# Attention decode with backward: one 2 MB store per outer product instead of two of 1 MB, and the V evacuation behind the p copy

## The chip, the cores and the metric

The kernel runs on one core of a Trainium2 chip. The metric is the device time of one execution in microseconds (us); each result was compared with runs of the kernel before on the same chip in the same rounds. The 16 DMA engines of the core play the main part. In the traces every transfer of the queue leaves 16 completion marks, one per engine, and the marks come in the order in which the transfers were issued: in the kernel before, none of 3328 marks lies ahead of the mark of the same rank of the transfer before it. So the text treats each engine as working through its own share in that order.

## The reference, cut to what matters

```python
B, H, Sq, Skv, Dh = 1, 32, 1, 8192, 128          # bf16
scores = einsum('bhqd,bhkd->bhqk', q, k) * Dh ** -0.5
attn   = softmax(scores)
out    = einsum('bhqk,bhkd->bhqd', attn, v)
# returned: out, and the gradients of q, k, v for a given grad_out
```

With one query row per head, the gradients of k and v are outer products: dk is ds times q, dv is p times grad_out, each as large as K itself. So a head reads K and V (2.1 MB each) and writes dk and dv (2.1 MB each), and does little arithmetic per byte.

## The kernel before: the parts concerned

The store of an outer product. VectorE makes a quarter per call (r = 0 to 3); after every second quarter a DMA of 1 MB is issued, 128 rows of 8 KB. The last head stores in quarters. All DMAs go through one queue (SyncE), in program order.

```python
NST = 2
def outer(h, which, r):
    ...
    nc.vector.tensor_tensor(slots(G, r, 4) ..., op=ALU.mult)
    parts = 4 if h == H - 1 else NST
    if r % (4 // parts) == 4 // parts - 1:
        c = r // (4 // parts)
        nc.sync.dma_start(rows_of(dst, h, c, parts), slots(G, c, parts))
```

The order of a head h (p_ is the head before). The K transpose `k_blocks(h + 1, 0)` waits for the next K load, and VectorE executes in this order, so dk's third and fourth quarters stand behind that wait:

```python
    k_scores(h); v_transposes(h, 1)
    ds_of(p_); outer(p_, "dk", 0); s_mask(h); s_swap(h); outer(p_, "dk", 1)
    k_blocks(h + 1, 0)                    # VectorE: waits for K of head h + 1
    ... mx, diag ...
    outer(p_, "dk", 2); outer(p_, "dk", 3); dq_of(p_)
    load_k(h + 2)                         # needs the buffer that dq_of frees
    ...
    v_transposes(h, 3)                    # 16 transposes on PE, one 1 us copy on ScalarE
    rinv = ...                            # VectorE
    x["p"] = ...                          # ScalarE: the p copy
    v_scores(h, 2); contract(Vt.pop(h), x["p"], ...)
    for r in range(4): outer(h, "dv", r)
    ...
    load_v(h + 2)
```

## Time and profile before

| | before |
|---|---|
| time, median of the first 3 runs | 674.32 us (672.83 to 674.49) |
| span of the profiled run | 672.6 us |
| one turn (head) in the middle | 20.45 us |
| DMA rate in the middle (164 to 629 us) | 410 GB/s |
| from the landing of the last K to the end | 43.4 us |

The lines behind this table stand in the prediction. One view more matters for what follows, the list of DMA issues: out<-in, engine, operation, count, KB of each, median us from issue to landing.

```profile
out_dram<-G_dv SPq DMA_DIRECT2D x62, 1024.0 KB, 11.8
out_dram<-G_dk SPq DMA_DIRECT2D x62, 1024.0 KB, 11.9
Vt<-in_v_dram SPq DMA_DIRECT2D x30, 2048.0 KB, 16.4
```

A landing here is the completion of the 16 engines. A 1 MB store needs about 2.5 us of an engine's time (8 packets of 309 ns).

### The profile page before, as it was taken

The numbers are of one execution on the slowest core, as the hardware profiler recorded it, in microseconds if no ns is written. First come the engines' busy times: TensorE is split into PE (matmuls) and PEld (weight loads), VectorE is DVE, ScalarE is ACT, GpSimd is POOL, SyncE is SP. The second block draws the span as 40 slices with busy tenths as digits, with TensorE's granted clock in tenths as the row PEclk, the third lists the DMA queues.
The fourth block names the chain that finished last, engine by engine and source line by source line (L and its number), as shares of the span: only waits on it lengthen the run. The fifth ranks groups of instructions, "written<-read, shape, count | busy, mean of one in ns | idle before, by whom it ended". The sixth has DMA issues, their size and how long they took to land.

```text
span 672.6 us, 23041 instructions
## 1 busy us (share of the span) xinstructions
PE 524.4 (78%) x10727; PEld 483.7 (72%) x10727; DVE 508.7 (76%) x658; ACT 172.4 (26%) x321; POOL 0.7 (0%) x6
## 2 busy tenths in 40 slices
PE   3788897878888787878787887878787888877783
PEld 3687786767777777777777777767777777777682
DVE  4678896777787877877777778768777678687766
ACT  1323322222222223222222222222222222222320
POOL 0000000000000000000000000000000000000000
PEclk9975656565555555555555555656556565566665
DMA  8899999999999999999999999999999999999976
GB/s 338 370 382 422 419 427 418 422 427 424 405 410 414 409 411 393 421 416 402 406 412 405 413 413 409 402 416 409 423 419 399 423 399 415 413 396 417 391 292 252
DMA packets 29808, 269.96 MB, mean 401 GB/s; under 512 B 3472, under 2 KB 3472, under 8 KB 6032
## 3 DMA queue, kind: packets, MB, share of 16 engines
q1 hardware_dynamic: 29712, 268.48, 97.6%
q8 instruction: 84, 1.38, 0.8%
q14 instruction: 12, 0.10, 0.0%
HBM read 134.23 MB, written 134.23 MB: 399 GB/s over the span
## 4 chain that ended last, share of the span: by engine, by line
DMA 64%; PE 23%; DVE 8%; ACT 3%; issue 1%; SPq 1%; ACTq 0%; DVEq 0%
DMA Kt<-in_k_dram 64%; PE dp_ps L185 8%; PE T_ps L168 5%; DVE XK_sb L133 5%; PE m_ps L256 3%; PE dp_ps L180 3%; ACT XT_sb L170 2%; PE m_ps L185 1%; PE s_ps L145 1%; DVE diag L254 1%; DVE G_dv L195 1%; DVE G_dk L195 1%; PE m_ps L276 0%; DVE mx L252 0%; ACT p_rep L282 0%
## 5 line engine op out<-in xcount | busy, mean ns | idle before, releaser
L168 PE MATMUL T_ps<-ident,Vt 128*128 128x128 bf16 x2048 | 238.3, 310 | 1.1 <-DMA Vt<-in_v_dram 1.1
L168 PEld LDWEIGHTS <-Vt 128*128 128x128 bf16 x2048 | 218.5, 150 | 7.0 <-issue 5.4
L170 ACT COPY XT_sb<-T_ps 128x1024 f32<-128x1024 f32 x128 | 129.5, 1012 | 334.2 <-PE T_ps L168 334.2
L195 DVE TENSOR_TENSOR G_dv<-p_rep,qd 128x2048 bf16<-128x2048 bf16 x128 | 148.2, 1221 | 77.5 <-ACT p_rep L282 63.4
L133 DVE STREAM_TRANSPOSE XK_sb<-Kt 128x1024 f32<-128x1024 f32 x128 | 155.1, 1230 | 57.2 <-DMA Kt<-in_k_dram 57.2
L195 DVE TENSOR_TENSOR G_dk<-ds_rep,qd 128x2048 bf16<-128x2048 bf16 x128 | 153.2, 1219 | 1.1
L180 PEld LDWEIGHTS <-XT_sb 128*128 128x128 bf16 x2048 | 72.5, 106 | 45.1 <-ACT XT_sb L170 43.8
L180 PE MATMUL dp_ps<-doT,XT_sb 128*128 128x1 bf16 x2048 | 75.1, 166 | 35.3 <-ACT XT_sb L170 35.3
L185 PE MATMUL m_ps<-p_rep,Vt 128*128 128x1 bf16 x2048 | 59.0, 165 | 37.0 <-ACT p_rep L282 37.0
L185 PEld LDWEIGHTS <-Vt 128*128 128x128 bf16 x2048 | 59.5, 104 | 39.0 <-issue 39.0
L145 PE MATMUL s_ps<-q_blk,XK_sb 128*128 128x4 bf16 x2048 | 59.1, 168 | 0.0
L185 PE MATMUL dp_ps<-ds_rep,Kt 128*128 128x1 bf16 x2048 | 58.2, 164 | 0.7 <-issue 0.5
L145 PEld LDWEIGHTS <-XK_sb 128*128 128x128 bf16 x2048 | 57.1, 104 | 0.0
L185 PEld LDWEIGHTS <-Kt 128*128 128x128 bf16 x2048 | 56.2, 101 | 0.8 <-issue 0.6
L256 PE MATMUL m_ps<-diag,ones_f 128*128 128x128 f32 x64 | 21.5, 431 | 38.1 <-DVE diag L254 38.1
L256 PEld LDWEIGHTS m_ps<-diag,ones_f 128*128 128x128 f32 x64 | 13.9, 270 | 45.1 <-DVE diag L254 45.1
L276 PEld LDWEIGHTS m_ps<-rs,ones_f 128*128 128x128 f32 x64 | 15.9, 309 | 25.2 <-ACT qd L211 25.2
L276 PE MATMUL m_ps<-rs,ones_f 128*128 128x1 f32 x64 | 18.6, 360 | 16.4 <-ACT qd L211 16.4
L224 ACT COPY dq_all<-dp_ps 128x1 f32<-128x1 f32 x32 | 5.1, 159 | 93.4 <-PE dp_ps L185 93.4
L151 DVE TENSOR_TENSOR sm<-s_ps,in_quad 128x256 f32<-128x256 f32 x32 | 13.6, 425 | 12.3 <-PE s_ps L145 12.3
L287 ACT COPY o_all<-m_ps 128x1 f32<-128x1 f32 x32 | 5.1, 159 | 61.8 <-PE m_ps L185 61.8
L291 PE MATMUL m_ps<-o_all,do_f 128*128 128x1 f32 x64 | 18.1, 352 | 0.0
(40 smaller groups left out, 160.2 us busy)
## 6 DMA issues: line engine op xcount, KB each, us to landing
Kt<-in_k_dram SPq DMA_DIRECT2D x31, 2048.0 KB, 15.9
out_dram<-G_dv SPq DMA_DIRECT2D x62, 1024.0 KB, 11.8
out_dram<-G_dk SPq DMA_DIRECT2D x62, 1024.0 KB, 11.9
Vt<-in_v_dram SPq DMA_DIRECT2D x30, 2048.0 KB, 16.4
Vt<-in_v_dram SPq DMA_DIRECT2D x8, 512.0 KB, 11.2
Kt<-in_k_dram SPq DMA_DIRECT2D x4, 512.0 KB, 5.2
out_dram<-G_dv SPq DMA_DIRECT2D x4, 512.0 KB, 3.4
out_dram<-G_dk SPq DMA_DIRECT2D x4, 512.0 KB, 4.6
```

Source lines behind the costliest of these rows:

```text
L133: nc.vector.transpose(XK[h][:, :, :, u, :], slots(Kt[h], u, NCH).rearrange("p g d -> p (g d)").bitcast(F32).rearrange("p (g w j) -> p g w ...
L145: nc.tensor.matmul(out[:, g, :], lhsT=cols[:, g, c // 2, c % 2], rhs=q_blk[:, h, c, :], start=(c == 0), stop=(c == 2 * NB - 1), skip_group ...
L151: nc.vector.tensor_tensor(x["sm"][:], x["s"][:, 0:NT].rearrange("p (a g) -> p a g", a=NQ).unsqueeze(2) .to_broadcast([P, NQ, NCH, CH]), in ...
L168: nc.tensor.transpose(T_ps[:, i, :], Vt[h][:, c * CH + i, :], ident[:])
L170: nc.scalar.copy(X.rearrange("p c s -> p (c s)").bitcast(F32), T_ps.rearrange("p c s -> p (c s)").bitcast(F32))
L180: nc.tensor.matmul(st[h]["dp"][:, n:n + 1], lhsT=X[:, i, :], rhs=doT[:, h:h + 1], start=True, stop=True, skip_group_check=True)
L185: nc.tensor.matmul(out_col, lhsT=Xt[:, n, :], rhs=rep[:, n, 0:1], start=(n == 0), stop=(n == NT - 1), skip_group_check=True)
L195: nc.vector.tensor_tensor(slots(G, r, 4).rearrange("p n (a b) -> p n a b", b=R), slots(rep, r, 4).unsqueeze(2).to_broadcast([P, Q, D // R, ...
L254: nc.vector.tensor_scalar(diag[:], ident_f[:], mx[:], scale, op0=ALU.mult, op1=ALU.mult)
L256: nc.tensor.matmul(x["m"][:, 128:256], lhsT=ones_f[:], rhs=diag[:], start=True, stop=True, skip_group_check=True)
L276: nc.tensor.matmul(x["m"][:, 0:1], lhsT=ones_f[:], rhs=rs[:], start=True, stop=True, skip_group_check=True)
L291: nc.tensor.matmul(x["m"][:, 1:2], lhsT=do_f[:, h:h + 1].to_broadcast([P, P]), rhs=o_all[:, h:h + 1], start=True, stop=True, skip_group_ch ...
```

## The change

Fewer and longer stores, and p earlier. The one part halves the number of store packets and DMAs; the other lets the p copy, on which V's contraction and the dv products wait, go ahead of a V evacuation on ScalarE.

```diff
-NST = 2
+NST = 1
@@
-        v_transposes(h, 3)
         rinv = small.tile([P, 1], F32, tag="rinv")
         ...
         x["p_s"] = small.tile([P, NT], F32, tag="p_s", name="p_s")
         nc.vector.tensor_scalar(x["p_s"][:], e[:], rinv[:], scale, op0=ALU.mult, op1=ALU.mult)
+        v_transposes(h, 3)
         v_scores(h, 2)
```

## The prediction

> **What bounds the kernel now.** I read the row of slices and the DMA queues on the page first, then the chain of waits in time order for two heads in the middle, then the busy time by stage, then the timeline of one head and of the last two.
>
> ```profile
> PE   3788897878888787878787887878787888877783
> ...
> DVE  4678896777787877877777778768777678687766
> ...
> DMA  8899999999999999999999999999999999999976
> ...
> q1 hardware_dynamic: 29712, 268.48, 97.6%
> ```
>
> No compute engine is full (PE and DVE stay at 6 to 8 tenths in all but one of the slices between the ends), the 16 DMA engines are at 9 from the third slice to the 38th, and the one data queue fills 97.6% of them. The chain that ended last says the same of a middle head:
>
> ```profile
> 304.74 15.76 DMA Kt<-in_k_dram
> 320.49 0.02 issue
> 320.52 1.25 DVE XK_sb L133
> 321.76 0.12 DVE mx L252
> 321.88 0.02 issue
> 321.91 0.30 DVE diag L254
> 322.20 0.04 issue
> 322.25 0.80 PE m_ps L256 x2
> 323.05 0.40 PE dp_ps L180 x16
> 323.45 1.71 PE dp_ps L185 x64
> 325.16 0.03 PE m_ps L207
> 325.19 15.85 DMA Kt<-in_k_dram
> ```
>
> One turn is 20.45 us: a 2 MB K load is issued and lands 15.8 us later, 4.7 us of compute follow until dq has freed a K buffer, and the next load goes out. The load takes so long because other transfers lie ahead of it in the queue: a head moves K, V, dk and dv, 8.39 MB, and 8.39 MB in 20.45 us is 410 GB/s. So a turn is DMA throughput, not latency. By stage (columns: PE, PEld, DVE, ACT, POOL busy us and instructions, then clock, DMA share, GB/s):
>
> ```profile
> 0.00:28.00 28.00, 14.05 (x225) 12.32 (x226) 13.04 (x28) 6.51 (x9) 0.70 (x6) 1.00 0.92 372
> 28.00:42.00 14.00, 12.37 (x276) 11.61 (x273) 13.62 (x18) 3.21 (x5) 0.00 (x0) 1.00 0.87 309
> 42.00:98.00 56.00, 47.51 (x994) 44.62 (x994) 46.22 (x60) 16.01 (x30) 0.00 (x0) 0.53 1.01 423
> 98.00:164.00 66.00, 51.20 (x1043) 47.19 (x1040) 49.84 (x64) 16.75 (x34) 0.00 (x0) 0.55 1.01 423
> 164.00:629.00 465.00, 372.56 (x7605) 343.26 (x7603) 356.52 (x450) 121.11 (x225) 0.00 (x0) 0.53 1.01 410
> 629.00:672.60 43.60, 26.75 (x604) 24.74 (x601) 29.42 (x41) 8.82 (x19) 0.00 (x0) 0.58 0.74 295
> ```
>
> The reader is to see two limits. From 42 to 629 us the DMA share is 1.01: only faster packets help there. From 629 us, where the last K has landed, the share is 0.74 and the chain is compute: a shorter path helps there. Between 28 and 42 us, when the first loads are done and the first outputs are not there yet, the DMA also waits a little (0.87).
>
> **What the Trainium skill says.** "DMA: Bandwidth & Descriptors", section "Why small descriptors are slow (HBM only)", gives each packet a fixed overhead of about 3 cycles and a fixed descriptor cost. The packet records of this trace agree that there is one and that it is small here: the median packet of 4096 bytes takes 159 ns, of 8192 bytes 309 ns, of 16384 bytes 611 ns. That is 150 ns per 4096 bytes plus about 9 ns per packet. The section "Rules for kernel authors" asks for 128 partitions and at least 1 MiB per DMA for full bandwidth; the stores before (1024 KB each in the list of DMA issues) already have that, so no jump is promised. The section "Where 436 GB/s comes from" puts the ceiling at 435.2 GB/s; the 423 of the best stage is 3% under it, so there is little above. "Perfetto Trace Analysis", section "Per-engine timelines", calls ScalarE a strict FIFO; the trace agrees: the p copy starts at 308.84 us, right behind a V evacuation at 307.93 us, though its scalar from the reciprocal was written at 306.55 us.
>
> **The change, part by part.** *Stores.* In 31 of 32 heads (the last stores in four parts before and after) dk and dv go from two 1 MB DMAs each to one of 2 MB. An engine writes 8 of the 128 rows, so per head it handles 32 packets of 8192 bytes before and 16 of 16384 after. The size of 16384 occurs only in loads before; I choose to apply the same law to stores, because the stores of 8192 lie on the line through the other two. Then 32 x 309 = 9888 ns become 16 x 611 = 9776 ns: 112 ns less. Two DMAs fewer also save two semaphore packets of 9 ns on each engine: 18 ns. Sum 130 ns per head, x 31 = **4.0 us**, all of it in the stretch that DMA bounds. The trigger moves: dv's first half waits for two more products (2 x 1.2 = 2.4 us), dk's for a K transpose and two products (318.85 to 324.4: 5.6 us). Does the queue run dry? The V load issued at 314.47 us takes 16.4 us to land, that is until 331, so the queue holds work when dk comes at 324.4; K, issued at 304.74 and landing at 320.5, covers dv at 314. No. The order of bytes in the queue (dv, V, dk, K) stays.
>
> *Buffers.* An output tile is rewritten two heads (41 us) later; a store landing some 14 us after its later issue is long done. No new wait. SBUF does not change.
>
> *V evacuation behind p.* The number of instructions is the same on every engine and the order on PE is the same; only on ScalarE do the 1.01 us copy (row of L170: 1012 ns) and the 0.51 us p copy change places, and on VectorE nothing but tags moves. The p copy no longer waits for 16 transposes (1.87 us) and the evacuation: it can start at about 306.6 instead of 308.84, so VectorE's dv products start 2.3 us earlier. On PE the contraction with V waited for p until 309.40; now it waits only for the scores before it, which end at 308.24: 1.15 us earlier. In the DMA-bound stretch both lie beside the transfers: zero. In the last 43.6 us they lie on the chain twice. Head 30: 1.15 us through PE. Head 31: here the chain runs from p into VectorE's eight products to the end, and VectorE stood idle for 2.74 us, so 2.3 us. The end of the chain moves by about 3.4 us; the DMA must then push out dk of head 30 (2 MB, one store at about 650) and 4 MB of head 31 by then: 6.3 MB at 410 GB/s are 15.4 us, so about 666, against some 669.5 before. Both agree; I take **3.3 us**.
>
> *Start.* dv of head 0 goes out at about 30.0 whole instead of 29.57 and 32.19 in halves, and V2 behind it some 2 us earlier. The gap from 28.3 us grows by 0.5, the later small gaps (0.4 at 36, 0.35 at 41 us) close, and the low rate around 35 to 42 us may improve: **0.5 to 1 us** gained.
>
> Sum: 4.0 + 3.3 + 0.7 = 8.0 us, 674.3 - 8.0 = 666.3 us.
>
> **The rivals.** (a) *Slow packets decide.* The loads' mean packet is 648 ns against the median 611, the stores' (8192) 316 against 309: 7892 x 37 / 16 + 15890 x 6.6 / 16 = 25 us per engine are spent in slow packets. From 98 to 164 us there are hardly any and the rate is 423; after 164 us, where half of the engines load while the other half store, it is 410. If the longer packets or the fewer DMA boundaries keep the engines in the good state, 465 us x (1 - 410/423) = 14 us more are saved: 652 us. If 16 KB stores get slow as often as the loads do (6% instead of 2% of some 305 us of store packets), 12 us are lost, and the time is 678. Nothing in the profile tells which; I think neither, as bytes and order in the queue stay. (b) *Later triggers starve the queue* (dk 5.6 us later). Against it is the backlog of some 14 us at K's issue; for it, only the start and the end, where there is no backlog: at the end dk of head 30 as one store leaves DMA idle from 646 to 650. That would eat 2 to 3 us of the tail: 669. (c) *The evacuation behind p becomes a wait*: scores of the fourth V part need it. They come on PE after the contraction of 1.84 us, and the evacuation ends about 308.9, before that: no wait. (d) *PE or DVE as bound*: in the first 98 us a head took about 18.5 us by the same chain, so compute allows 18.5 us against DMA's 20.45; the change only lowers it. No.
>
> **Range and chances.** The certain terms are small: packets 4, tail 2 to 3.5, start 0 to 1. The uncertain one is (a), some 12 us either way with about one chance in six for a large part of it, more likely as a gain since fewer and longer transfers are less mixed. The 2% line is 660.8 us, 5.5 us under my number, and needs a visible gain in slow packets. I give 0.17 to faster, 0.80 to same, 0.03 to slower, and a range of 656 to 673.
>
> **What would show it.** Right: store packets of 16384 bytes with a median near 611 ns; half of the store issues at 2048 KB; a middle turn of 20.3 us with K still waited for; DMA share still 1.01 with 411 to 414 GB/s in the middle; the p copy ahead of the evacuation and the contraction 1.15 us earlier against the row sums' matmul; some 40 us instead of 43.6 from the last K landing to the end. Wrong: a middle rate far from 410 (then rival a, to be seen in mean minus median of the packets), DMA share under 1.0 in the middle (rival b), or a new wait of PE on the evacuation (rival c).

## The result and the profile after

The changed kernel is slower: 681.52 us in the median of 4 runs (679.74 to 683.2), the kernel before 674.4 us. The ratio is 1.0106 with a 95% interval of 1.0073 to 1.0140. That is within 2%, but clear of noise, outside the predicted range, and on the other side.

The page of the changed kernel, rows of the slices and the data queue:

```profile
DMA  8899999999999999999999999999999999999978
...
q1 hardware_dynamic: 20784, 268.48, 97.8%
```

The packets fell from 29712 to 20784 as meant, and the queue is as full as before. Next the stages (PE, PEld, DVE, ACT, POOL busy us with counts, then clock, DMA share, GB/s):

```profile
28.00:42.00 14.00, 12.29 (x250) 11.39 (x248) 13.08 (x18) 3.92 (x8) 0.00 (x0) 1.00 0.82 324
...
98.00:164.00 66.00, 52.02 (x1083) 48.16 (x1084) 50.66 (x67) 16.33 (x30) 0.00 (x0) 0.50 1.00 406
164.00:629.00 465.00, 363.88 (x7495) 336.25 (x7492) 352.92 (x447) 122.20 (x227) 0.00 (x0) 0.54 1.00 403
```

The start moved a little more data (324 against 309 GB/s). The loss is in the middle: 406 instead of 423 and 403 instead of 410 GB/s, at the same busy share. The engines are as busy and move less, so their packets take longer. The chain of waits of one turn:

```profile
310.27 16.46 DMA Kt<-in_k_dram
326.73 0.02 issue
326.76 1.25 DVE XK_sb L133
...
329.38 1.71 PE dp_ps L185 x64
331.09 0.08 PE m_ps L207
331.17 16.16 DMA Kt<-in_k_dram
```

A turn is 20.9 us here (310.27 to 331.17), and K takes 16.2 us to land in the median instead of 15.9. The last K landed at 639.78 us instead of 629.15: 10.6 us later. From there to the end it took 40.2 us (680.0 - 639.78) instead of 43.4, 3.2 us less, as predicted. The moved evacuation did its part too; in the timeline the p copy now follows its reciprocal at once, and dv's products follow the p copy:

```profile
311.95 0.13 DVE L279 RECIPROCAL rinv<-m_ps 128x1 f32<-128x1 f32 x1
312.11 0.51 ACT L281 ACTIVATE p_rep<-e,rinv 128x256 bf16<-128x256 f32 x1 [1.11 <-DVE rinv L279]
...
312.65 4.63 DVE L195 TENSOR_TENSOR G_dv<-p_rep,qd 128x2048 bf16<-128x2048 bf16 x4 [0.28 <-ACT p_rep L281]
```

What the page does not show, the packet records of the traces do. Per engine (sums over all packets, divided by 16):

| | before | after | difference |
|---|---|---|---|
| all packets | 661.9 us | 670.3 us | +8.4 |
| the same packets at the median of their size (611, 309, 159, 9 ns) | 635.7 us | 631.7 us | -4.1 (rounded) |
| the rest: what packets took beyond their median | 26.2 us | 38.7 us | +12.5 |

So the sum of the packets' usual times fell as predicted, by 4.1 us against 4.0, and 12.5 us of slow packets came on top, which the prediction had put at zero. (Not all of the 4.1 us is time won: on an engine the next packet's record starts some 3 to 4 ns before the last one ends, and with fewer packets these overlaps fell from 6.04 to 4.66 us per engine.) A slow packet is no rare hiccup: about one in ten of the 16384-byte packets takes 12% or more beyond 611 ns, mostly 0.7 to 1.3 us in all. Before, the share was the same, but then only the loads had this size.

### The profile page after: what moved, and what is told of

Read it like the earlier page. It is cut to its first block, busy times and chain, and to the rows that moved or that the text cites. A ratio compares the mean times of both kernels' runs of the same rounds, so it can differ in the third digit from the quotient of the medians.

```text
span 680.0 us, 22883 instructions
## 1 busy us (share of the span) xinstructions
PE 522.9 (77%) x10727; PEld 482.8 (71%) x10727; DVE 508.7 (75%) x658; ACT 175.7 (26%) x321; POOL 0.7 (0%) x6
## 3 DMA queue, kind: packets, MB, share of 16 engines
q1 hardware_dynamic: 20784, 268.48, 97.8%
## 4 chain that ended last, share of the span: by engine, by line
DMA 71%; PE 17%; DVE 9%; ACT 1%; SPq 1%; issue 1%; DVEq 0%
DMA Kt<-in_k_dram 71%; PE dp_ps L185 8%; DVE XK_sb L133 5%; PE m_ps L256 3%; PE dp_ps L180 2%; PE T_ps L168 2%; DVE diag L254 1%; DVE G_dv L195 1%; DVE G_dk L195 1%; DVE mx L252 1%; PE s_ps L145 1%; PE m_ps L185 1%; SPq L81 0%; ACT XT_sb L170 0%; SPq L75 0%
## 5 line engine op out<-in xcount | busy, mean ns | idle before, releaser
L168 PEld LDWEIGHTS <-Vt 128*128 128x128 bf16 x2048 | 216.5, 149 | 8.1 <-issue 5.7
L256 PE MATMUL m_ps<-diag,ones_f 128*128 128x128 f32 x64 | 23.3, 464 | 84.6 <-DVE diag L254 84.6
L185 PEld LDWEIGHTS <-Vt 128*128 128x128 bf16 x2048 | 57.1, 104 | 0.0
L281 ACT ACTIVATE p_rep<-e,rinv 128x256 bf16<-128x256 f32 x32 | 16.2, 507 | 37.2 <-DVE rinv L279 37.2
## 6 DMA issues: line engine op xcount, KB each, us to landing
Kt<-in_k_dram SPq DMA_DIRECT2D x31, 2048.0 KB, 16.2
out_dram<-G_dk SPq DMA_DIRECT2D x31, 2048.0 KB, 11.5
Vt<-in_v_dram SPq DMA_DIRECT2D x8, 512.0 KB, 12.5
```

Source lines behind the costliest of these rows:

```text
L168: nc.tensor.transpose(T_ps[:, i, :], Vt[h][:, c * CH + i, :], ident[:])
L185: nc.tensor.matmul(out_col, lhsT=Xt[:, n, :], rhs=rep[:, n, 0:1], start=(n == 0), stop=(n == NT - 1), skip_group_check=True)
L256: nc.tensor.matmul(x["m"][:, 128:256], lhsT=ones_f[:], rhs=diag[:], start=True, stop=True, skip_group_check=True)
L281: nc.scalar.activation(x["p"][:], e[:].unsqueeze(2).to_broadcast([P, NT, R]), ACT.Copy, scale=rinv[:])
```

## The experiments

Two theories were sent first. **A**: long store packets (16 KB rows) are slow. **B**: the single trigger comes late. A third, **C**, blamed the moved evacuation.

### The two parts one by one

`e1_nst1_only` has NST = 1 in the kernel before; `e2_vmove_only` has NST = 2 in the changed kernel.

> Stores as one 2 MB DMA, V evacuation left where it was. If the 16 KB store packets are slow (theory A) or the late single trigger is (theory B), this is as slow as the changed kernel plus the tail's 3 us: 682 to 686 us, middle rate 400 to 406 GB/s. If the earlier p copy shifts the phase of the DMA (theory C), this is as fast as the kernel before or a little faster: 668 to 674 us, middle rate 410 or more.

> V evacuation moved behind the p copy, stores as two halves as before. Theories A and B: the tail's 3 us are gained and nothing lost: 670 to 672 us. Theory C: the loss is here: 680 us or more, middle rate near 403 GB/s.

Measured: one store with the old order 677.82 us (ratio 1.0068, interval 1.0033 to 1.0103); moved evacuation with two stores **667.89 us** (0.9916, 0.9886 to 0.9947). So C falls, the loss comes with the single store, and the moved evacuation alone is a gain of about 6 us, more than the 3 us expected: its tail is 40.2 us like the changed kernel's, its start (28 to 42 us) runs at 351 GB/s instead of 309, its middle at 411. e1 was outside the expected 682 to 686: its packets were hardly slower (28.0 us beyond the median), but its engines had less work: of its span of 678.3 us, packets fill 659.6, so 18.7 us are empty, against 10.7 before. Of these 8 us more, 3.4 lie at the start (28 to 42 us); the middle is nearly unharmed (before: 309 and 410 GB/s):

```profile
28.00:42.00 14.00, 12.36 (x273) 11.67 (x273) 13.11 (x17) 3.68 (x6) 0.00 (x0) 0.53 0.63 234
164.00:629.00 465.00, 367.44 (x7528) 338.74 (x7529) 355.36 (x451) 120.54 (x227) 0.00 (x0) 0.54 1.00 409
```

The single store costs either idle time or slow packets.

### An experiment that tested nothing, and one that split the loads

`e3_late_halves` was to issue two halves late:

```diff
-        if r % (4 // parts) == 4 // parts - 1: ...
+        elif r == 3:
+            for c in range(2):
+                nc.sync.dma_start(rows_of(dst, h, c, 2), slots(G, c, 2))
```

> As the changed kernel, but each output goes out as two DMAs of 8 KB rows, both issued after the fourth product. Theory A (packet size): 670 to 673 us, mean store packet of 8192 bytes near 316 ns. Theory B (late, bunched trigger): near 680 us with slow packets also among those of 8192 bytes.

Measured: 668.96 us (0.9934). I first read this as a proof of A. It is none. The queue waits for the data of each DMA only, and no other instruction stands between the two on the queue, so moving the line in the program moved nothing: in the trace the first dk half goes out at 317.54 us, the second at 324.07. The run is a repetition of e2.

`e4_loads_8k` is the changed kernel with `parts = ... else 2` in both load functions.

> As the changed kernel, but K and V loads in two DMAs of 8 KB rows, so that loads (8192) and stores (16384) can be told apart in the packet records. Theory A: stores of 16384 have a mean of 640 ns or more, loads of 8192 some 315 to 320 ns, time near that of the kernel before (672 to 678 us), since only one side is long. Theory B: stores near 620, loads of 8192 6 per cent over their median (327 ns), time 680 us.

Measured: 673.59 us (1.0004). Stores of 16384 bytes took 634 ns in the mean and the loads, now of 8192, took 327 instead of a median of 309: neither pattern as expected. The short loads were as slow as B said, the stores in between, and the time lies in A's range. This did not decide.

### Which store, and which length

`e8_dv_16k` and `e9_dk_16k` store one output whole and the other in halves, with the moved evacuation (`1 if which == "dv" else 2`, and the reverse). `e5_two_dmas_16k` stores 16 KB rows by two DMAs of 64 partitions, `e6_stores_4k` by four DMAs of 4 KB rows.

> Earlier p copy, dv stored by one 2 MB DMA of 16 KB rows, dk in halves of 8 KB rows. If every long store packet costs the same: half of the 13.6 us between the two kernels, 673 to 676 us. If the loss sits at the passage from K load to dv store (where the slow stores of the run with 8 KB loads lay): 679 to 683 us.

> Earlier p copy, dk stored by one 2 MB DMA of 16 KB rows, dv in halves of 8 KB rows. If every long store packet costs the same: 673 to 676 us. If the loss is dv's alone: 665 to 668 us, a little under the run with the moved evacuation alone.

> As the changed kernel (16 KB rows), but each output in two DMAs of 64 partitions, 1 MB each, issued together after the fourth product. If the length of the rows (the packet of 16384 bytes) makes the stores slow, this stays near the changed kernel, 677 to 683 us, excess of the 16384 packets about 6 per cent of the middle. If the size or the number of the DMAs does, it is near the run with late halves, 667 to 671 us. It also pairs rows and engines differently, so a result outside both ranges would speak for that.

> As the changed kernel, but each output in four DMAs of 4 KB rows, all issued after the fourth product. Dose: if the excess of store packets grows with their length it should fall from 1.0 per cent of the middle (8 KB) to about 0.5 per cent here, while 64 x 159 - 32 x 309 ns are 0.29 us per head more of base time: 672 to 677 us. If length does not matter below 8 KB the excess stays 1.0 per cent and the time is 676 to 680 us.

Measured: dv whole 668.85 us (0.9919), dk whole **682.39 us** (1.0114), two DMAs of 64 partitions 775.79 us (1.1512), 4 KB rows 685.72 us (1.0181). All four missed what was expected. dv in 16 KB rows costs nothing and dk in 16 KB rows costs all of it, so the length of the rows is not the cause (A falls): both outputs have the same shape and rows. The 4 KB rows are not faster either; what their loads took beyond the median rose. The 64-partition run is a case of its own: the Trainium skill, "DMA: Bandwidth & Descriptors", "Rules for kernel authors", advises against two transfers to partition halves; it says that they serialize. Here the run took 94 us more than the changed kernel that it was made from, so it does not speak on A or B.

What differs between dk and dv is *when* they are issued against the queue's work. That brought me to the completion marks of the 16 engines, which the trace holds one by one.

### The sixteen engines are not level

The same skill page, section "Why a DMA increments its semaphore by 16 and not by 1", says that a DMA runs on up to 16 engines that finish independently. The traces agree, and by much more than I had assumed. Completion of each engine, in us, for the V load and the dk store behind it (issue times first):

```
before  V  314.47  324.2 324.3 324.5 324.7 324.7 325.0 325.0 327.9 328.3 328.7 330.0 330.0 330.0 330.1 330.3 330.8
        dk 318.85  326.6 326.7 ...                                                                333.6 (1st half)
        dk 324.49  329.2 329.3 ...                                                                336.2 (2nd half)
after   V  317.75  331.8 331.9 332.0 332.0 332.1 332.1 332.2 332.6 333.0 333.2 333.8 334.8 335.1 335.3 336.1 336.9
        dk 330.73  337.5 337.7 ...                                                                342.2
```

Before, seven engines run 3 to 7 us ahead of the others. In the changed kernel the V load's first engine is done at 331.8 us, and dk was issued at 330.73, only 1.1 us earlier; at the start of the run the first packet of a store follows its issue by 0.84 us. The leading engines' dk takes 5.5 us instead of 4.9 (first landing of V to first landing of dk, median of the heads issued from 200 to 600 us, as in the rest of this part).

It looks as if they ran dry and waited for the store. The packet records of the trace show something else. In this turn the leading engines start dk within 0.15 us of V's last packet, and from dk's issue to 335 us all 16 together stand without a packet for 0.23 us. What they lose comes at the end of dk: six packets that start between 336.13 and 336.38 us take 1208 ns, about twice 611. From 164 to 629 us there are 95 packets of this length (within 2 ns), 90 of them 5 to 6 us after dk's issue, 3.5 us per engine in all; the fast run f3 below has 97. In the fast run e11 there are 47, and 42 stand 5 to 6 us after the issue of dv, which there is the store with the least work ahead. So a mark of the late trigger is there, but it is small. In the issues of the queue (start, us, engine, line), the changed kernel:

```profile
317.75 0.38 SPq L81 DMA_DIRECT2D Vt<-in_v_dram  x1
330.73 0.34 SPq L203 DMA_DIRECT2D out_dram<-G_dk  x1
331.17 0.38 SPq L75 DMA_DIRECT2D Kt<-in_k_dram  x1
```

and its list of DMA issues:

```profile
out_dram<-G_dv SPq DMA_DIRECT2D x31, 2048.0 KB, 14.4
out_dram<-G_dk SPq DMA_DIRECT2D x31, 2048.0 KB, 11.5
```

A 2 MB store needs 4.9 us of an engine, so dk has 11.5 - 4.9 = 6.6 us of earlier work in front of it on the slowest engine, dv 9.5. Counted directly from the marks, from an issue to the moment when the slowest engine is done with the transfer ahead, the medians are 6.2 us for dk and 9.1 for dv. I call this a store's **head start**. Before, the shortest of the four stores' head starts was 8.8 us (dv's first half; dk's halves had 12.2 and 9.0). The head start seems to bound how far the leading engines can run ahead: in eleven of the first fourteen runs of the table below they land the transfer ahead 1.2 to 2.0 us after the issue of the store with the shortest head start, however long that is. The time between first and last landing of a K load fell from 6.9 us to 4.3.

### Late with short rows, early with long rows

This gives theory **T** (the late trigger of dk), against **R** (something in dk's 16 KB rows themselves). `e10_dk_late_halves` keeps 8 KB rows and makes them late by issuing the second half first, so that the queue's order holds back the other:

```diff
+        if which == "dk" and h < H - 1:
+            if r == 3:
+                for c in (1, 0):
+                    nc.sync.dma_start(rows_of(dst, h, c, 2), slots(G, c, 2))
+            return
```

`e11_dk_early_16k` keeps the 2 MB stores and moves dk's last two products ahead of the K transpose, where VectorE was idle anyway (3.7 us in the turn shown above); `e12_dk_early_8k` is the same with NST = 2:

```diff
             outer(p_, "dk", 1)
+            if more:
+                outer(p_, "dk", 2)
+                outer(p_, "dk", 3)
@@
-            outer(p_, "dk", 2)
-            outer(p_, "dk", 3)
+            if not more: ...              # the last head as before
```

`e13_kbufs4` is the changed kernel with K_BUFS = 4 and `load_k(h + 3)`.

> Earlier p copy, all stores in halves of 8 KB rows, but dk's second half is issued first, so that both dk DMAs go out only after the fourth product (in the earlier run named late halves the queue's order let the first half go early, so that run only repeated the moved evacuation). Theory T (late trigger: the fastest engines reach dk less than 1.6 us after its issue and stall): slow as with dk in 16 KB rows, 679 to 684 us, first to last landing of a DMA 4 to 5 us instead of 7. Theory R (16 KB rows of dk themselves): 667 to 669 us as with the moved evacuation alone.

> The changed kernel (2 MB stores of 16 KB rows), with dk's third and fourth products moved ahead of the K transpose that waits for the K load, so that dk is issued some 4 to 5 us earlier. Theory T: the loss goes away, margin of the fastest engine 5 us or more, 662 to 668 us. Theory R: stays at 678 to 683 us.

> As the run before with early dk, but stores in halves of 8 KB rows. Theory T: the second dk half also gets its margin (1.8 us in the moved-evacuation run): 663 to 668 us, within 4 us of the 16 KB version and not faster than it by more than 2. Theory R: 665 to 669 us, 12 us or more faster than the 16 KB version.

> The changed kernel with a fourth K buffer and K loaded three heads ahead: one more load stands in the queue, about 5 us more of backlog. Theory T: dk's margin grows by up to 5 us and the loss goes away: 662 to 669 us. Theory R: 678 to 683 us.

Measured: late with 8 KB rows **682.52 us** (1.0117, 1.0094 to 1.0140); early with 16 KB rows **668.71 us** (0.9920, 0.9898 to 0.9941); early with 8 KB rows 669.05 us (0.9924); four K buffers 668.03 us (0.9905). That is T in all four, though e11 and e12 lie 0.7 and 1.1 us above its ranges, and R is out. (e10 also swaps the order of the halves in memory; e11 and e13 do not, and agree.) In e13 dk's head start grew to 9.7 us, but the expected margin did not come: the leading engines reached dk 1.8 us after its issue and had run further ahead. The list of DMA issues for dk, first of the late halves, then of the early whole store:

```profile
out_dram<-G_dk SPq DMA_DIRECT2D x62, 1024.0 KB, 9.7
```

```profile
out_dram<-G_dk SPq DMA_DIRECT2D x31, 2048.0 KB, 16.1
```

and the middle stage of the same two runs:

```profile
164.00:629.00 465.00, 361.84 (x7478) 335.00 (x7479) 351.67 (x446) 121.44 (x224) 0.00 (x0) 0.55 1.01 403
```

```profile
164.00:629.00 465.00, 371.23 (x7607) 342.54 (x7604) 363.68 (x455) 123.73 (x225) 0.00 (x0) 0.53 1.01 414
```

The late short rows run at the changed kernel's 403 GB/s, the early long ones at 414. Time beyond the median per engine: 37.2 and 23.9 us. In e10 loads and stores can be told apart by size: against e2, which differs only in dk's issue, the loads' time beyond the median in the middle rose from 13.5 to 16.9 us, the stores' from 4.8 to 9.3. Both got slower. The number of packets, by contrast, is worth nothing that can be told once the trigger is in time (668.71 against 669.05 us): of the 4 us less of base time 2.1 went into slow packets (23.9 against 21.8) and 2.0 into empty time (11.5 against 9.5).

### Dose, the other store, and both cures

Four more runs: `f3_dk_half_early` moves only dk's third product (dk is issued one product earlier); `f4_early_16k_oldorder` is e11 with the evacuation back in its old place; `f1_early_16k_kbufs4` and `f2_early_8k_kbufs4` join early dk and four K buffers.

> Dose of lateness: 16 KB stores, K in 3 buffers, only the third dk product moved ahead of the K transpose, so dk is issued about 1.2 us earlier than in the changed kernel (margin about 2.5 to 2.7 us instead of 1.5). If the stall is a threshold near 1 us after the issue, the loss is gone: 668 to 671 us. If the loss is gradual: 672 to 678 us.

> 16 KB stores with early dk products, V evacuation back ahead of the p copy. It tells whether the moved evacuation costs something by itself with one store per output: by the tail alone this is 3 to 5 us slower than with the moved evacuation (671 to 675 us). If the stores' lateness and the move are independent, its distance to the kernel with one store and the old order (677.8) is as large as between 681.5 and 668.7, so 665 us; that I do not expect, as dv then has a margin of under 1.9 us.

> 16 KB stores, early dk products and a fourth K buffer. If the late trigger was the loss, both cures together give no stall at all: 664 to 668 us, and it should be the fastest. If what is left is slow packets alone, it stays at 667 to 669 us like each cure by itself.

> As the run before with halves of 8 KB rows. The prediction of 4 us for fewer packets would put it 3 to 5 us above the 16 KB version; if the 16 KB stores give that back in slow packets, within 1.5 us of it.

Measured: f3 670.4 us (0.9949): 1.2 us of earlier issue bring back nearly all. But not as expected by a larger margin for the leading engines: that stayed at 1.4 us, and they ran further ahead instead (first to last landing of K 5.5 us). f4 688.57 us (1.0211): slow again, though dk is early; here dv is the late one, with a head start of 6.7 us. I had expected 671 to 675. f1 687.71 us (1.0185), f2 671.11 us (0.9956): joining the cures is worse than each alone, and f1 is 17 us slower than f2, where at most 1.5 us were expected: a clear miss.

All runs that speak on it, ordered by the shortest head start of a store (median in us, from the completion marks; empty is the span less the packets' time; the ratio is to the kernel before of the same rounds), and below them three runs with other loads, rows or partitions:

| run | rows of dk / dv | shortest head start | beyond the median, us per engine | empty, us | ratio |
|---|---|---|---|---|---|
| one store, old order (e1) | 16 / 16 KB | 5.9 (dk; dv 6.8) | 28.0 | 18.7 | 1.0068 |
| changed kernel | 16 / 16 | 6.2 (dk) | 38.7 | 9.7 | 1.0106 |
| dk whole (e9) | 16 / 8 | 6.2 (dk) | 40.0 | 8.4 | 1.0114 |
| dk late halves (e10) | 8 / 8 | 6.2 (dk) | 37.2 | 8.1 | 1.0117 |
| early dk, old order (f4) | 16 / 16 | 6.7 (dv) | 37.9 | 15.9 | 1.0211 |
| dk one product earlier (f3) | 16 / 16 | 7.3 (dk) | 26.9 | 9.3 | 0.9949 |
| dv whole (e8) | 8 / 16 | 8.7 (dv) | 24.7 | 6.8 | 0.9919 |
| before | 8 / 8 | 8.8 (dv) | 26.2 | 10.7 | 1 |
| moved evacuation (e2) | 8 / 8 | 8.8 (dk) | 25.7 | 5.8 | 0.9916 |
| early dk (e11) | 16 / 16 | 8.9 (dv) | 23.9 | 11.5 | 0.9920 |
| four K buffers (e13) | 16 / 16 | 9.7 (dk) | 25.6 | 9.5 | 0.9905 |
| early dk (e12) | 8 / 8 | 11.2 (dv) | 21.8 | 9.5 | 0.9924 |
| early dk, four K buffers (f1) | 16 / 16 | 11.6 (dv) | 28.6 | 21.0 | 1.0185 |
| early dk, four K buffers (f2) | 8 / 8 | 12.7 (dv) | 21.3 | 13.9 | 0.9956 |
| loads in two DMAs (e4) | 16 / 16 | 8.9 (dk) | 30.3 | 6.1 | 1.0004 |
| four DMAs of 4 KB rows (e6) | 4 / 4 | 11.3 (dk) | 35.1 | 2.0 | 1.0181 |
| two DMAs of 64 partitions (e5) | 16 / 16 | 7.1 (dk) | 118.7 | 21.8 | 1.1512 |

Among the first fourteen every run with 6.7 us or less loses, and from 7.3 us on every run but f1 gains over the kernel before, whatever the rows. (e3, the same as e2, is left out.) But the head start is not the whole cause. e1 has the shortest and hardly more slow packets than the kernel before. The last three have 7.1 us and more and do not gain; e6 pays 10 us of base time for its short packets, but also 9 us more beyond the median. And f1, with 11.6 us, begins as one of the fastest and falls off, in two stretches of its middle:

```profile
164.00:400.00 236.00, 185.46 (x3884) 171.31 (x3881) 182.10 (x230) 62.02 (x113) 0.00 (x0) 0.57 1.00 415
400.00:625.00 225.00, 169.09 (x3469) 155.25 (x3467) 166.41 (x209) 57.18 (x106) 0.00 (x0) 0.55 0.99 393
```

while the first and last landing of K drift from 6 to 12 us apart. Its loss is mostly empty time, 21.0 us against 9.5 to 11.5 with each cure alone, and less slow packets. Why it falls off is open.

## Why the prediction was wrong, point by point

**What bounds the kernel** (DMA throughput to 629 us, then the chain): right. Every term could be read off again in the changed profile.

**Packets, 4.0 us**: right as a sum of packet times. The 16384-byte stores do have a median of 611 ns, and the base time fell by 4.1 us; but 1.4 us of it were overlaps of successive records, so that an estimate of the time won is 2.7 us.

**Tail, 3.3 us**: right; 3.2 us, and 40.2 us from the last K landing to the end where 40 were named.

**Start, 0.5 to 1 us**: about right in size; 324 instead of 309 GB/s in 14 us are 0.2 MB, 0.5 us at 410 GB/s. Not by closing gaps, though: from 28 to 42 us the engines stood without a packet for 2.5 us instead of 1.8, and lost 1.0 us instead of 2.0 in slow packets.

**The p copy and the evacuation, no new wait**: right on the path that it describes. Outside the tail the move was put at zero; alone (e2) it gained about 6 us, the tail's 3.2 and most of the rest at the start, where the engines stood empty for 0.4 us instead of 1.8.

**Slow packets: "I think neither, as bytes and order in the queue stay."** This is the step that failed. The term was put at zero and measured 12.5 us. Bytes and order did stay, but the time at which dk is issued did not, and with the late trigger packets got slower. Rival (a) named the size (12 us, 678 us in all), but by luck, as its cause was the length of the packets; the 8 KB rows issued late were as slow (682.52 us).

**"Does the queue run dry? ... No."** The answer itself held: between 164 and 629 us the engines stood without a packet for 1.0 us each, against 0.6 before. What failed is the step from there to no cost, in rival (b) too, which knew a late trigger only as a starved queue, at the start and the end. The check compared dk's later issue with the landing of the V load, 16.4 us after its issue, which is the landing of the slowest engine; the leading engines are done some 6 us before that. With dk's trigger 5.6 us later the shortest head start fell from 8.8 us (dv's first half) to 6.2 (dk), and the loss came in the middle, as slow packets in a full queue.

**The sum.** -4.1 and +12.5 for the packets are +8.4 us, and the empty time of the engines fell by 1.0 us only, from 10.7 to 9.7, so the span rose by 7.4 us (680.0 - 672.6). Without a packet the engines stood 3.6 us less from 629 us on, but 0.7 us more at the start and 0.6 us more from 98 to 629 us; the 1.4 us of overlaps that fell away count as empty time too.

**What is shown and what is not.** Shown: in the kernel with the moved evacuation the time of dk's trigger decides, not the rows (e10 against e2, e11 against the changed kernel). In f4 it is dv that comes late, and the run is as slow; there 5 us more of empty time come on top. Shown: with a late trigger the engines move closer together (first to last K landing 4.3 to 5.3 us; 8 to 10 engines within 1 us of the first instead of 7), more packets are slow (in all but e1), and the K load takes the slowest engine 5.4 to 5.6 us instead of 4.9 in the three kernels with a late dk and moved evacuation. Not shown: *why* packets are slower with a late trigger. The leading engines' loss on dk by itself is not it, since it is as large in f3 (dk 5.6 us), which is fast. That engines run close together is not enough either: in the kernel before, the K loads issued from 42 to 80 us have their first and last landing only 1.9 to 2.2 us apart, and from 42 to 98 us packets lost 1.6% of the time beyond their median (423 GB/s), against 6.3% in the middle of the changed kernel. Also open: why one store with the old order (e1) pays in idle time and not in slow packets, why f1 falls off, and why e4 and e6 have slow packets.

## What to carry to other kernels

A transfer lands when its slowest engine is done, so issue-to-landing times overstate the backlog of the leading engines: before delaying a trigger, look at the completion of all 16 engines and at the store's head start (here 6.7 us or less lost, and 7.3 or more gained in most runs). A full queue is not the whole check: the loss came as slower packets, with the engines hardly ever idle. Merging two stores into one saves packets but delays the first half by the time of the products it waits for; pair it with moving those products ahead of a wait. Of the versions tried, moving the p copy alone (667.89 us), or adding early dk products or a fourth K buffer to the change (668.71 and 668.03 us), beat both kernels; they are within noise of each other.

## What the Trainium skill lacked or had wrong

- "DMA: Bandwidth & Descriptors" says that the engines of one DMA finish independently, but not how far apart: here the first and the last of 16 engines landed the same 2 MB load 6.9 us apart in the steady state, more than the 4.9 us that the load takes one engine, and up to 12 us with early dk and a fourth K buffer.
- The same page gives no figure for packets beyond their usual time beside other traffic: here, from 164 to 629 us, some 4% of the engines' time in good runs and near 6% in bad ones, 410 to 414 against 403 GB/s, with the engines equally busy. Mean minus median of the packets shows it.
- Its rule of at least 1 MiB per DMA is met by both kernels. No page says what waiting for more data costs when two such DMAs are made one: nothing between 1 and 2 MB where the trigger is in time (669.05 against 668.71 us), about 13 us where it is late (681.52 against 667.89 us).
- Its advice against splitting a transfer into partition halves agrees, but is too mild: it calls it no use, and here it cost 14% against the changed kernel that has one store (775.79 against 681.52 us, of different rounds).
